# Attention with top-32 masking and two expert layers: three weight loads moved in SP's queue, and the first tiles' bound array made by ScalarE and TensorE

## The chip, the core and the metric

One core of a Trainium2 chip runs the whole program; the metric is the device time of one execution in microseconds (us). The engines are PE (TensorE, matrix products; PEld is its weight load), DVE (VectorE), ACT (ScalarE), POOL (GpSimd) and SP (SyncE, which here only issues DMAs). Each engine runs its own instructions in order, and they wait for each other by semaphores.

## The reference

Batch 4, 8 heads, 576 tokens, head size 64. Each query keeps its 32 highest scores; then a dense two-layer block, then a layer of eight experts of which each token takes one.

```python
scores = scale * np.matmul(q, k.transpose(0, 1, 3, 2))
kth = np.partition(scores, -top_k, axis=-1)[..., -top_k:-top_k + 1]
attn = softmax(np.where(scores >= kth, scores, -1e9))   # top_k = 32
x = (attn @ v) as 2304 tokens x 512
h = x @ w_in;  x = (h * np.clip(h + 3, 0, 6) / 6) @ w_out     # 512 -> 2048 -> 512
e = argmax(x @ w_gate);  out = gate * (np.maximum(x @ w1[e], 0) @ w2[e])
```

The dense block's weights come as 64-bit floats, and the kernel makes 32-bit ones of them itself.

## The kernel before, in words

The program has three stages that overlap. The **attention** runs over 144 tiles of 128 queries by 576 keys. The **dense block** runs over 144 groups (9 blocks of 256 tokens by 16 slices of the hidden layer), about one group for each tile as soon as a block of tokens is there; the rest of the groups follows the last tile. Then come the **experts**.

One attention tile t goes through these steps. `qk` (line 630) makes the scores in `sps` on PE; `sevac` copies them to `sbuf` on ACT (line 300, a helper's line), of which there are five. `top_a` takes on DVE the eight best of each eighth (line 660, tile `cd`) and from those the 24 best in three rounds (lines 666 and 671, tiles `m` and `cw`). `top_c` makes a bound `u` just under the 24th best (ACT, line 684). Then the scores above `u` are taken out and the best eight of what is left are found: `z8` (line 731, DVE). From tile 20 on (`ZPE = 20`) DVE takes them out in SBUF (`top_z`, line 696). For the first 20 tiles, when PE and the PSUM space `yps2` of the dense block are free, PE does it: `z_pe` lets POOL write an array `zw` (line 703) that holds -2^100 where the score is above `u` and 0 elsewhere, and `qk(t, zw)` makes the scores a second time in `yps2`, with the array added by a product with an identity, `identb`. That is this text's "second score product".

`act_sign` (line 721, ACT) counts for every tile how many scores lie above `u`: it writes sign(u - s) into `jk` and sums it into `sg`. `mask` compares `sg` with a table (line 735) to see which of the eight is the 32nd best, and zeroes the weights below it (line 739). Then follow the transposes (`ptps`, line 755), the product with the values (line 789) and the evacuation (lines 802 to 839).

Beside this run **32 conversions** of weight pieces, `conv64`: SP loads a 512 KB piece into `raw` (three buffers, line 316), ACT squares it and takes a sign in `sq` (lines 328 and 333), DVE builds the 32-bit words in `cvs` by three instructions (lines 329, 336 and 339), and POOL splits them (lines 298 and 347). About one conversion goes with each tile. The first three loads carry a tiny POOL copy from the scores of tile 0 (line 315), which keeps them from starting before those are there.

The order on each engine is made by the Tile scheduler from priorities: `pr(name)` sets `tc.cur_priority` to the place in the loop plus a number from the table `PRIO`, and the lowest goes first among what is ready in its plan. So a changed dependency moves rows on every engine.

Of the kernel before, what the change touches and what calls it, by code (L numbers as in the profile page):

```python
# [13 lines left out]
F32 = mybir.dt.float32  # L14
F32R = mybir.dt.float32r
BF16 = mybir.dt.bfloat16
# [41 lines left out]
def attention_two_moe_kernel(  # L58
# [95 lines left out]
    def pr(name, least=0):  # L154
        tc.cur_priority = max(least, pr0[0] + PRIO[name])
# [72 lines left out]
    def body(cs, exact, ends=None):  # L228
# [79 lines left out]

        def conv64(src, a_, nm, parts):
            n_ = DM // a_  # L310
            pr("load", pbase + 8 * len(wload))
            raw = m1p.tile([P, a_, n_, 2], U32, tag="ysb", bufs=NRAW, name=f"raw{nm}")
            if nm in ("i0", "o0", "i1"):

                G.tensor_copy(raw.rearrange("p a n t -> p (a n t)").bitcast(F32)[:, 0:1], ts[0]["s"][:, 0:1])
            SP.dma_start(raw.rearrange("p a n t -> p a (n t)"), src)
            yield
            lo, hi = raw[:, :, :, 0], raw[:, :, :, 1]
            wf = m1p.tile([P, DM], F32, tag="cvs", bufs=3, name=f"cv{nm}").rearrange("p (a n) -> p a n", a=a_)
            wb = wf.bitcast(U32)  # L320
            hf = hi.bitcast(F32)
            sq = ap1.tile([P, S], F32 if exact else BF16, tag="z" if exact else "jk", bufs=2 if exact else 1,
                          name=f"sq{nm}")[:, 0:DM].rearrange("p (a n) -> p a n", a=a_)
            pr("conv")
            if CSQ:
                G.tensor_tensor(sq, hf, hf, op=ALU.mult)
            else:
                A.activation(sq, hf, AF.Square)
            V.tensor_scalar(wb, hi, 3, 0x3FFFFFFF, op0=ALU.logical_shift_left, op1=ALU.bitwise_and)
            if not exact:  # L330
                i = wcnt[0]
                wcnt[0] += 1
                A.activation(sq, sq, AF.Sign, bias=cs["ntiny"], scale=1.0, accum_out=csum[:, i:i + 1])
            yield
            pr("conv")
            V.scalar_tensor_tensor(wb, hi, 0xC0000000, wb, op0=ALU.bitwise_and, op1=ALU.bitwise_or)
            yield
            pr("conv")
            V.scalar_tensor_tensor(wb, lo, 29, wb, op0=ALU.logical_shift_right, op1=ALU.bitwise_or)
            if exact:  # L340
                G.tensor_scalar(sq, sq, TINY2, None, op0=ALU.is_ge)
                G.tensor_tensor(wf, sq, wf, op=ALU.mult)
            yield
            pr("conv")
            h, l, done = parts()
            copy(CH, h, wf)
            G.tensor_tensor(l, wf, r_(h), op=ALU.subtract)
            done()
# [34 lines left out]
        def conv_upto(i):  # L383
            while cdone[0] <= i:
                run(conv_next())
# [1 line left out]

        identb = []
        if not exact:
            identb.append(ap1.tile([P, P], BF16, name="identb"))  # L390
            G.tensor_copy(identb[0], ident)
        NPB, NSB, VB = 3, 3 + LA, 2


# [210 lines left out]
        def qk(t, zw=None):  # L605
            pr("qk" if zw is None else "zpe")
            n, o = tiles[t]
            b, p = visits[n][:2]
            st = qx[n]
            kt = kx[b, p]  # L610
            for half in range(2):
                dst = (sps if zw is None else yps2)[:, half, 0:HS]
                if o == "T":

                    fw = visits[n][3] // P * P
                    mm = []
                    for i in st:
                        mm.append((dst, i[:, 0, fw:fw + P], kt[0][:, half * HS:(half + 1) * HS]))
                        a_, b_ = half * HS, min((half + 1) * HS, N4)
                        mm.append((dst[:, 0:b_ - a_], i[:, 1, fw:fw + P], kt[1][:, TAIL + a_:TAIL + b_]))  # L620
                        if half:
                            mm.append((dst[:, b_ - a_:HS], i[:, 1, fw:fw + P], kt[1][:, 0:TAIL]))
                else:
                    h, j = o
                    js = slice(j * P, (j + 1) * P)
                    mm = [(dst, i[:, h, js], kt[h][:, half * HS:(half + 1) * HS]) for i in st]
                if zw is not None:
                    mm.insert(0, (dst, identb[0], zw[:, half * HS:(half + 1) * HS]))
                for i, (d_, a_, b_) in enumerate(mm):
                    PE.matmul(d_, a_, b_, start=(i == 0), stop=(i == len(mm) - 1))  # L630

# [66 lines left out]
        def z_pe(t):  # L698
            if exact or not 0 <= t < ZPE:
                return  # L700
            pr("zw")
            zw = ap1.tile([P, S], F32, tag="z", bufs=2, name=f"z{t}").bitcast(BF16)[:, 0:S]
            G.tensor_scalar(zw, ts[t]["s"][:, 0:S], ts[t]["u"], -HUGE, op0=ALU.is_gt, op1=ALU.mult)
            qk(t, zw)

        def act_exp(t):
            pr("exp")
# [6 lines left out]
        def act_sign(t):  # L714
            if exact:
                return
            pr("sign")
            d = ts[t]
            jk = ap1.tile([P, S], BF16, tag="jk", bufs=1, name=f"jk{t}")
            d["sg"] = ap1.tile([P, 1], F32, tag="sg", bufs=3, name=f"sg{t}")  # L720
            A.activation(jk, d["s"][:, 0:S], AF.Sign, bias=ts[t]["u"], scale=-1.0, accum_out=d["sg"])  # L721

        def mask(t):
            if not 0 <= t < T:
                return
            d = ts[t]
            if not exact:
                pr("max8")
                z8 = ap1.tile([P, 8], F32, tag="z8", bufs=3, name=f"z8_{t}")
                j8 = ap1.tile([P, 8, 2], F32, tag="j8", bufs=1, name=f"j8_{t}")  # L730
                V.max(z8, d["z"])  # L731
                A.activation(zall[:, t:t + 1], z8[:, 1:2], AF.Sign, bias=ts[t]["u"], scale=-1.0)
                yield
                pr("match")
                V.scalar_tensor_tensor(j8, psum_isum, d["sg"], z8.unsqueeze(2).to_broadcast([P, 8, 2]), op0=ALU.is_equal, op1=ALU.mult,  # L735
                                       accum_out=tall[:, t:t + 1])
                yield
            pr("mask")
            V.scalar_tensor_tensor(d["p"], d["s"], tall[:, t:t + 1], d["p"], op0=ALU.is_ge, op1=ALU.mult)  # L739
            if tiles[t][1] == "T":  # L740

                lo, hi = d["pb"][:, N4:S], d["pb"][:, S:SW]
                copy(True, hi[TAIL:P], lo[TAIL:P])
                G.memset(lo[TAIL:P], 0.0)
                G.memset(hi[0:TAIL], 0.0)
            yield
# [355 lines left out]
        for t in range(T + 7):  # L1102
# [17 lines left out]
                pv(t - 5)  # L1120
            if t + LA < T:
                sevac(t + LA)
            if 0 <= t - 5 < T:
                xevac(t - 5)
            xg = None
# [334 lines left out]
```

## Time and profile before

| | before |
|---|---|
| median of 3 runs | 1199.83 us (1197.64 to 1202.85) |
| the profiled execution's own time | 1204.39 us |
| its span | 1202.5 us |
| busy share PE / DVE / ACT / POOL | 93% / 78% / 67% / 38% |
| POOL's array pass of the first 20 tiles | 48.6 us of POOL's busy time |
| last mask of the attention starts at | 863.3 us |

The profile's first part gives each engine's busy time. The windows view cuts the span into stretches with their own busy times and TensorE clock (granted share: 1.00 is 2.4 GHz, and values between 0.5 and 1 are stretches that mix the levels of 1.2 and 2.4 GHz). The timeline lists instructions by time, with the idle time of the engine before each in brackets and what ended it.

### The profile page before, as it was taken

The page shows a single profiled execution, that of the slowest core. Times are in us where ns is not written, and L with a number is a line of the kernel's source. Part 1 is how long each engine was busy: PE and PEld are TensorE (multiplying, and loading weights), DVE is VectorE, ACT ScalarE, POOL GpSimd, SP SyncE. Part 2 cuts the span into 40 slices and gives each one's busy share as a digit, 9 for nine tenths or more (in the row PEclk, how much of TensorE's full clock was granted, in tenths as well). Part 3 has the DMA queues.
Part 4 walks back from the last instruction along what each step waited for, and adds up shares of the span by engine and source line. Part 5 has one row for each costly group of instructions (what it writes and reads, how often), then busy time and mean ns, then how long its engine had stood idle before and what let it go on. Part 6 is the DMA issues. An engine that isn't in the chain of part 4 may idle for free.

```text
span 1202.5 us, 24061 instructions
## 1 busy us (share of the span) xinstructions
PE 1118.5 (93%) x7414; PEld 1003.8 (83%) x7414; DVE 940.9 (78%) x3853; ACT 807.6 (67%) x2082; POOL 458.5 (38%) x668
## 2 busy tenths in 40 slices
PE   5677688999999999999999999999999899999995
PEld 4566577778999989999988899999888799888885
DVE  5989989999999999998999899999641554545540
ACT  4777877778878788778778788777541353444441
POOL 5877646644332354433342432322344311222110
PEclk9668879999999999999999999999999899999998
DMA  3654456564553555754444554543486555455530
GB/s 76 189 179 142 143 171 221 162 174 125 157 134 113 151 134 142 177 135 135 118 122 126 133 147 125 152 133 110 127 271 163 176 187 179 161 176 185 160 121 31
DMA packets 184123, 179.24 MB, mean 149 GB/s; under 512 B 123629, under 2 KB 148509, under 8 KB 183984
## 3 DMA queue, kind: packets, MB, share of 16 engines
q1 hardware_dynamic: 178960, 167.24, 48.3%
q0 software_dynamic: 3872, 10.08, 2.6%
q8 instruction: 61, 1.00, 0.4%
q14 instruction: 78, 0.64, 0.2%
q10 hardware_dynamic: 1152, 0.28, 0.1%
HBM read 159.53 MB, written 18.61 MB: 148 GB/s over the span
## 4 chain that ended last, share of the span: by engine, by line
PE 71%; DVE 16%; issue 5%; ACT 4%; POOL 2%; DMA 2%; SPq 0%; POOLq 0%; ACTq 0%; DVEq 0%
PE l1ps L863 15%; PE yps L894 13%; PE ptps L789 9%; PE lp L1263 8%; PE ops L1286 8%; PE sps L630 6%; PE ptps L755 4%; DVE cd L660 2%; DVE pbuf L739 2%; DVE z L696 2%; DVE z L731 1%; PE ptps L935 1%; DVE m L666 1%; DVE cw L671 1%; PE misc L474 1%
## 5 line engine op out<-in xcount | busy, mean ns | idle before, releaser
L894 PE MATMUL yps<-wo,gh 128*128 128x512 f32 x544 | 206.7, 418 | 0.1
L298 POOL TENSOR_SCALAR gh<-gf 128x256 fp32r<-128x256 f32 x144 | 72.7, 505 | 345.2 <-PE yps L894 196.0
L660 DVE MAX8 cd<-sbuf 128x8 f32<-128x72 f32 x1152 | 187.9, 218 | 3.4 <-ACT sbuf L300 3.2
L863 PE MATMUL l1ps<-xh,wih 128*128 128x256 f32 x576 | 167.6, 291 | 4.7 <-DVE gf L875 3.1
L863 PE MATMUL l1ps<-xh,wil 128*128 128x256 f32 x576 | 164.0, 285 | 0.0
L863 PE MATMUL l1ps<-xl,wih 128*128 128x256 f32 x576 | 163.9, 285 | 0.0
L789 PE MATMUL ptps<-vn,pt 128*128 128x65 f32 (+1 forms) x1152 | 145.8, 281 | 0.0
L789 PEld LDWEIGHTS ptps<-vn,pt 128*128 128x128 f32 x1152 | 143.0, 201 | 0.0
L739 DVE SCALAR_TENSOR_TENSOR pbuf<-sbuf,tall,pbuf 128x576 f32<-128x576 f32 x144 | 136.8, 950 | 0.1
L883 POOL TENSOR_TENSOR gl<-gf,gh 128x256 fp32r<-128x256 f32 x144 | 125.5, 871 | 11.4
L863 PEld LDWEIGHTS l1ps<-xh,wih 128*128 128x128 f32 x576 | 110.4, 192 | 14.9 <-DVE gf L875 7.6
L1036 DVE TENSOR_TENSOR wl<-raw,wh 128x1024 fp32r<-128x1024 f32 x64 | 78.6, 1236 | 53.7 <-ACT wh L1035 51.6
L721 ACT ACTIVATE jk<-sbuf,uall 128x576 bf16<-128x576 f32 x144 | 111.6, 775 | 4.2 <-DVE j L735 0.9
L863 PEld LDWEIGHTS l1ps<-xl,wih 128*128 128x128 f32 x576 | 110.6, 192 | 4.2
L712 ACT ACTIVATE pbuf<-sbuf,nb 128x576 f32<-128x576 f32 x144 | 111.2, 775 | 4.1 <-PE ptps L757 0.9
L894 PEld LDWEIGHTS yps<-wo,gh 128*128 128x128 f32 x544 | 101.2, 190 | 14.8 <-POOL qh L486 0.3
L300 ACT ACTIVATE sbuf<-sps 128x576 f32<-128x576 f32 x144 | 92.9, 645 | 30.4 <-PE sps L630 16.5
L869 ACT ACTIVATE gf<-l1ps,three 128x256 f32<-128x256 f32 x144 | 67.9, 471 | 66.9 <-PE l1ps L863 55.7
L755 PE MATMUL ptps<-ident,pbuf 128*128 128x128 f32 x576 | 93.9, 286 | 19.7 <-DVE j L735 12.6
L894 PE MATMUL yps<-wo,gl 128*128 128x512 f32 x272 | 110.4, 406 | 0.6 <-POOL gl L883 0.6
L863 PEld LDWEIGHTS l1ps<-xh,wil 128*128 128x128 f32 x576 | 110.6, 192 | 0.1
L630 PE MATMUL sps<-kx,qh 128*128 128x288 f32 (+2 forms) x336 | 96.8, 319 | 14.3 <-ACT sbuf L300 10.5
(259 smaller groups left out, 2974.7 us busy)
## 6 DMA issues: line engine op xcount, KB each, us to landing
wo<-wod SPq DMA_DIRECT2D x144, 512.0 KB, 3.8
raw<-in_moe_w_dram SPq DMA_DIRECT2D x64, 512.0 KB, 4.3
vn<-in_v_dram SPq DMA_DIRECT2D x96, 128.0 KB, 2.7
rawi<-in_moe_w_in_dram SPq DMA_DIRECT2D x16, 512.0 KB, 4.0
rawo<-in_moe_w_out_dram SPq DMA_DIRECT2D x16, 512.0 KB, 4.6
wod<-wc SPq DMA_DIRECT2D x16, 512.0 KB, 5.6
qn<-in_q_dram SPq DMA_DIRECT2D x126, 64.0 KB, 2.5
yd<-y SPq DMA_DIRECT2D x18, 258.0 KB, 5.1
```

The lines of the kernel that those rows point to most:

```text
L630: PE.matmul(d_, a_, b_, start=(i == 0), stop=(i == len(mm) - 1))
L660: V.max(cd[:, c, :], s[:, c * CK:(c + 1) * CK])
L712: A.activation(d["p"], d["s"], AF.Exp, bias=d["nb"], scale=SCALE)
L721: A.activation(jk, d["s"][:, 0:S], AF.Sign, bias=ts[t]["u"], scale=-1.0, accum_out=d["sg"])
L739: V.scalar_tensor_tensor(d["p"], d["s"], tall[:, t:t + 1], d["p"], op0=ALU.is_ge, op1=ALU.mult)
L755: PE.transpose(ptps[:, c * P:(c + 1) * P], pb[:, c0 + c * P:c0 + (c + 1) * P], ident)
L789: PE.matmul(d_, a_, b_, start=(i == 0), stop=(i == len(mm) - 1))
L863: PE.matmul(dst, a[:, c, fs], b_[:, c, :], start=(n == 0), stop=(n == 3 * NCC - 1))
L883: G.tensor_tensor(gl, gf, r_(gh), op=ALU.subtract)
L894: PE.matmul(acc(bk, tt), a[:, tsl], b_, start=(f == 0 and m == 0), stop=(f == NF1 - 1 and m == 2))
L1263: PE.matmul(lp, a[:, c, fs], b_[:, c, 0:w], start=(n == 0), stop=(n == 3 * NCC - 1))
L1286: PE.matmul(ops_[j][0:n], a, b_[:, ns], start=(f == 0 and i == 0), stop=(f == NF2 - 1 and i == len(ms) - 1))
```

## The change

Five edits. (1) Pieces `i0`, `o0` and `i1` are loaded at a priority ahead of everything else in the load class, and their conversions are called in the first round of the loop, at the priority `match`. A tiny POOL copy from the scores of tile 2 now holds their `cvs` and `sq` buffers until that tile is there. (2) `sq` lies in the two buffers tagged `z` and no longer in the one buffer of `jk`. (3) For tiles 0 to 19, POOL's array pass is gone. PE reads `jk` in its place: -2^99 times a field of ones (`below`) plus 2^99 times sign(u - s) gives 0 for a score under the bound and -2^100 for one above it. There are now four products for each half of the second score product, where there were three. (4) The sign pass of those tiles takes the priority `zw`. (5) The comparison with the table uses one column in place of two for those tiles.

```diff
         def conv64(src, a_, nm, parts):
             n_ = DM // a_
-            pr("load", pbase + 8 * len(wload))
+            early = nm in ("i0", "o0", "i1")
+            pr("load", 0 if early else pbase + 8 * len(wload))
+            if early:
+                tc.cur_priority -= 100
             raw = m1p.tile([P, a_, n_, 2], U32, tag="ysb", bufs=NRAW, name=f"raw{nm}")
-            if nm in ("i0", "o0", "i1"):
-
+            if early:
                 G.tensor_copy(raw.rearrange("p a n t -> p (a n t)").bitcast(F32)[:, 0:1], ts[0]["s"][:, 0:1])
...
-            sq = ap1.tile([P, S], F32 if exact else BF16, tag="z" if exact else "jk", bufs=2 if exact else 1,
-                          name=f"sq{nm}")[:, 0:DM].rearrange("p (a n) -> p a n", a=a_)
-            pr("conv")
+            sq = ap1.tile([P, S], F32, tag="z", bufs=2, name=f"sq{nm}")
+            sq = (sq if exact else sq.bitcast(BF16))[:, 0:DM].rearrange("p (a n) -> p a n", a=a_)
+            ck = "match" if early else "conv"
+            if early:
+                pr("load")
+                for x in (wf, sq):
+                    G.tensor_copy(x.rearrange("p a n -> p (a n)")[:, 0:1], ts[2]["s"][:, 0:1])
+            pr(ck)
...
-            identb.append(ap1.tile([P, P], BF16, name="identb"))
-            G.tensor_copy(identb[0], ident)
+            for i, a_ in enumerate((HUGE / 2, -HUGE / 2)):
+                identb.append(ap1.tile([P, P], BF16, name=f"identb{i}"))
+                G.tensor_scalar(identb[i], ident, a_, 0.0, op0=ALU.mult, op1=ALU.add)
+            below = ap1.tile([P, HS], BF16, name="below")
+            G.memset(below, 1.0)
...
-                    mm.insert(0, (dst, identb[0], zw[:, half * HS:(half + 1) * HS]))
+                    mm[0:0] = [(dst, identb[1], below), (dst, identb[0], zw[:, half * HS:(half + 1) * HS])]
...
-            pr("zw")
-            zw = ap1.tile([P, S], F32, tag="z", bufs=2, name=f"z{t}").bitcast(BF16)[:, 0:S]
-            G.tensor_scalar(zw, ts[t]["s"][:, 0:S], ts[t]["u"], -HUGE, op0=ALU.is_gt, op1=ALU.mult)
-            qk(t, zw)
+            qk(t, ts[t]["jk"])
...
-            pr("sign")
+            pr("sign" if t >= ZPE else "zw")
...
+                w_ = 1 if t < ZPE else 2
...
+            if t == 0:
+                conv_upto(1)
```

**Where rows move on DVE, start of the program.** Before, between the rounds of tile 1 (`m_1`, `cw_319`) and the first `z8` (`z_0`), only the eighths of tile 2 (`cd_395`) stood:

```order
L666 MAX m_1_317<-cw_319 128x8
L660 MAX cd_395<-sbuf_158 128x8
L671 MATCH_REPLACE cw_319<-m_1_317,cw_319 128x64
L660 MAX cd_395<-sbuf_158 128x8
L666 MAX m_1_317<-cw_319 128x8
L660 MAX cd_395<-sbuf_158 128x8 x6
L731 MAX z_0_406<-yps 128x8
```

Now the conversions of three pieces (`cvi_269`, `cvi_361`, `cvo_282`) stand there; these are the first rows of it, and the last:

```order
L676 MAX m_1_349<-cw_351 128x8
L336 TENSOR_SCALAR cvi_269<-rawi_236 128x512
L681 MATCH_REPLACE cw_351<-m_1_349,cw_351 128x64
L343 SCALAR_TENSOR_TENSOR cvi_269<-rawi_236,cvi_269 128x512
L676 MAX m_1_349<-cw_351 128x8
L346 SCALAR_TENSOR_TENSOR cvi_269<-rawi_236,cvi_269 128x512
L336 TENSOR_SCALAR cvi_361<-rawi_242 128x512
...
L346 SCALAR_TENSOR_TENSOR cvo_282<-rawo_239,cvo_282 128x512
L670 MAX cd_429<-sbuf_162 128x8 x4
L738 MAX z_0_440<-yps 128x8
```

So nine DVE instructions moved ahead of the first `z8`.

**Where rows move on SP's queue.** Before, the last load of the second pair's queries (`qn_222`) stood right behind that pair's keys (`kd_1`), then seven loads of values, the third pair's keys and queries, and only then the first two weight pieces:

```order
L515 DMA kd_1_208<-in_k_dram 128x4x64 x2
L528 DMA qn_222<-in_q_dram 128x2x64
L549 DMA vn_161<-in_v_dram 128x4x64
...
L515 DMA kd_2_293<-in_k_dram 128x4x64 x2
L516 DMA ke_2_294<-in_k_dram 64x64 x2
L528 DMA qn_370<-in_q_dram 128x2x64 x4
L550 DMA vp_164<-in_v_dram 64x64
L316 DMA rawi_232<-in_moe_w_in_dram 128x4x256
L316 DMA rawo_235<-in_moe_w_out_dram 128x1024
```

Now three pieces stand behind `kd_1`, and the last load of the second pair's queries (`qn_226`) stands behind the third pair's keys (`kd_2`, `ke_2`):

```order
L525 DMA kd_1_212<-in_k_dram 128x4x64 x2
L318 DMA rawi_236<-in_moe_w_in_dram 128x4x256
L318 DMA rawi_242<-in_moe_w_in_dram 128x4x256
L318 DMA rawo_239<-in_moe_w_out_dram 128x1024
L559 DMA vn_165<-in_v_dram 128x4x64
L525 DMA kd_2_325<-in_k_dram 128x4x64 x2
L526 DMA ke_2_326<-in_k_dram 64x64 x2
L538 DMA qn_226<-in_q_dram 128x2x64
```

The weight pieces moved ahead by two pairs' loads, and one load of queries moved back behind four loads of keys.

## Rows read from the trace of the kernel before

**Rows 1.** Windows view; columns: stretch, length, busy PE, PEld, DVE, ACT, POOL, clock, DMA.

```profile
15.00:33.00 18.00, 14.10 (x58) 11.08 (x59) 12.94 (x74) 11.24 (x29) 12.77 (x13) 0.91 0.46 120
33.00:60.00 27.00, 15.48 (x76) 13.26 (x75) 27.00 (x71) 21.09 (x53) 23.80 (x22) 0.69 0.64 175
60.00:150.00 90.00, 65.21 (x376) 56.06 (x376) 83.38 (x346) 72.86 (x192) 63.44 (x46) 0.78 0.52 155
300.00:860.00 560.00, 553.72 (x4068) 510.77 (x4068) 521.37 (x2442) 444.32 (x1246) 192.15 (x319) 1.00 0.51 136
```

**Rows 2.** Timeline of DVE, 18 to 36 us: start, duration, instruction, idle before.

```profile
18.28 0.21 DVE L666 MAX8 m<-cw 128x8 f32<-128x64 f32 x1
...
22.22 0.77 DVE L731 MAX8 z<-yps 128x8 f32<-128x576 f32 x1 [2.93 <-PE yps L630]
...
28.64 0.77 DVE L731 MAX8 z<-yps 128x8 f32<-128x576 f32 x1 [0.94 <-PE yps L630]
...
32.58 0.24 DVE L660 MAX8 cd<-sbuf 128x8 f32<-128x72 f32 x1 [0.66 <-ACT sbuf L300]
...
33.45 0.89 DVE L329 TENSOR_SCALAR cvi<-rawi 128x512 uint32<-128x512 uint32 x1
...
34.40 0.67 DVE L336 SCALAR_TENSOR_TENSOR cvi<-rawi,cvi 128x512 uint32<-128x512 uint32 x1
...
35.17 0.71 DVE L339 SCALAR_TENSOR_TENSOR cvi<-rawi,cvi 128x512 uint32<-128x512 uint32 x1
```

**Rows 3.** DMA issues: size of one, median us from issue to landing.

```profile
rawi<-in_moe_w_in_dram SPq DMA_DIRECT2D x16, 512.0 KB, 4.0
...
qn<-in_q_dram SPq DMA_DIRECT2D x126, 64.0 KB, 2.5
```

**Rows 4.** Timeline of SP's queue, 13 to 26 us.

```profile
13.14 0.62 SPq L528 DMA_DIRECT2D qn<-in_q_dram  x1
...
23.11 1.22 SPq L515 DMA_DIRECT2D kd<-in_k_dram  x2
```

**Rows 5.** Groups of instructions, 0 to 150 us, shapes apart: busy us, mean ns | idle before.

```profile
L703 POOL TENSOR_SCALAR z<-sbuf,uall 128x576 bf16<-128x576 f32 x20 | 48.6, 2429 | 10.6 <-ACT uall L684 9.3
...
L329 DVE TENSOR_SCALAR cvi<-rawi 128x512 uint32<-128x512 uint32 x10 | 7.6, 758 | 0.0
```

**Rows 6.** Timeline of POOL and then DVE, 97 to 106 us.

```profile
97.44 2.21 POOL L703 TENSOR_SCALAR z<-sbuf,uall 128x576 bf16<-128x576 f32 x1
...
102.16 1.28 POOL L347 TENSOR_TENSOR wil<-cvi,wih 128x512 fp32r<-128x512 f32 x1
103.54 2.77 POOL L703 TENSOR_SCALAR z<-sbuf,uall 128x576 bf16<-128x576 f32 x1
...
97.58 0.87 DVE L329 TENSOR_SCALAR cvi<-rawi 128x512 uint32<-128x512 uint32 x1
...
99.05 0.80 DVE L739 SCALAR_TENSOR_TENSOR pbuf<-sbuf,tall,pbuf 128x576 f32<-128x576 f32 x1
...
102.59 1.47 DVE L739 SCALAR_TENSOR_TENSOR pbuf<-sbuf,tall,pbuf 128x576 f32<-128x576 f32 x1
...
105.39 0.40 DVE L329 TENSOR_SCALAR cvo<-rawo 128x512 uint32<-128x512 uint32 x1
```

**Rows 7.** DVE's groups with idle time before them, 15 to 150 us.

```profile
L839 DVE TENSOR_TENSOR xl<-misc,xh 128x128 fp32r<-128x128 f32 x8 | 2.3, 284 | 4.1 <-ACT xh L835 4.1
...
L802 DVE TENSOR_SCALAR rs<-ptps 128x2 f32<-128x2 f32 x8 | 1.2, 151 | 2.5 <-PE ptps L789 2.5
```

**Rows 8.** Timeline of ACT and then PE, 114 to 117 us.

```profile
114.25 0.78 ACT L721 ACTIVATE jk<-sbuf,uall 128x576 bf16<-128x576 f32 x1
...
114.72 0.46 PE L630 MATMUL yps<-z,identb 128*128 128x288 bf16 x1
...
115.47 0.46 PE L630 MATMUL yps<-z,identb 128*128 128x288 bf16 x1
...
116.21 1.06 PE L755 MATMUL ptps<-ident,pbuf 128*128 128x128 f32 x4
```

More of the change, by code (lines that the diff above doesn't have):

```diff
@@ L334, in conv64 @@
             yield
-            pr("conv")
+            pr(ck)
             V.scalar_tensor_tensor(wb, hi, 0xC0000000, wb, op0=ALU.bitwise_and, op1=ALU.bitwise_or)
             yield
-            pr("conv")
+            pr(ck)
             V.scalar_tensor_tensor(wb, lo, 29, wb, op0=ALU.logical_shift_right, op1=ALU.bitwise_or)
@@ L716, in act_sign @@
                 return
-            pr("sign")
+            pr("sign" if t >= ZPE else "zw")
             d = ts[t]
-            jk = ap1.tile([P, S], BF16, tag="jk", bufs=1, name=f"jk{t}")
+            d["jk"] = jk = ap1.tile([P, S], BF16, tag="jk", bufs=1, name=f"jk{t}")
             d["sg"] = ap1.tile([P, 1], F32, tag="sg", bufs=3, name=f"sg{t}")
@@ L734, in mask @@
                 pr("match")
-                V.scalar_tensor_tensor(j8, psum_isum, d["sg"], z8.unsqueeze(2).to_broadcast([P, 8, 2]), op0=ALU.is_equal, op1=ALU.mult,
-                                       accum_out=tall[:, t:t + 1])
+                w_ = 1 if t < ZPE else 2
+                V.scalar_tensor_tensor(j8[:, :, 0:w_], psum_isum[:, :, 0:w_], d["sg"], z8.unsqueeze(2).to_broadcast([P, 8, w_]),
+                                       op0=ALU.is_equal, op1=ALU.mult, accum_out=tall[:, t:t + 1])
                 yield
```

## The prediction

> **What bounds the kernel now.** I read the windows view first, because the share of the whole span says little about a kernel of three stages [rows 1]. From 300 to 860 us PE is busy 553.7 of 560 us at the full clock and DVE 521.4. From 33 to 60 us DVE is busy 27.0 of 27 us, while PE has 15.5. From 60 to 150 us it is DVE 83.4 and PE 65.2 of 90. So the first 150 us, where the change lies, are DVE's, and PE waits there. The order of the tiles is fixed and each tile brings one group of the dense block with it, so what DVE loses or gains before 150 us shifts everything after it. I count the change in DVE's busy and idle time, and nothing that it does to POOL alone.
>
> Second, the timeline of DVE at the start [rows 2]. DVE is through with tile 1's rounds at about 18.5 us and then waits: 2.93 us for the first `z8` at 22.22, 0.94 us for another at 28.64, and 0.66 us for scores at 32.58. That is 4.5 us. The first conversion comes only at 33.45, and from there on DVE has no hole for 27 us. The wait at 22.22 ends with PE's second score product, which waited for POOL's array pass.
>
> **Three conversions into the holes.** One conversion takes DVE 0.89 + 0.67 + 0.71 = 2.27 us [rows 2], three take 6.8 us. The order of the changed kernel puts them between tile 1's rounds and the first `z8`. Are the pieces there? A 512 KB load lands a median 4.0 us after its issue [rows 3]. SP comes to the first of them where it issued the last queries before, at 13.14 us; each issue holds the queue for 0.62 us [rows 4]. POOL's small copy must come first and needs tile 0's scores, which were there at about 13.5. So the first lands at about 13.8 + 4.0 = 17.8 us, and the others by 20. DVE gets to them at 18.5, 20.8 and 23, so it should wait for none. It then has work from 18.5 to at least 26.5 (6.8 us plus the eighths of tile 2, some 1.2 us), while the first `z8` is ready at about 22: the hole of 2.93 us is gone.
>
> What is late next is the moved load of queries. It now stands behind the third pair's keys, which SP issued at 23.11, when PE had read the keys before them [rows 4]; four key loads take 2.4 us, the query load 0.6, and it lands 2.5 us later [rows 3], at about 28.7. PE transposes it then, ACT and DVE split it at about 30. DVE has `z8`, masks and eighths of tiles 2 and 3 to fill the time up to there, about 3.4 us from 26.5 on, so I leave a hole of 0.5 us. The term is 4.5 - 0.5 = **-4.0 us**. Its ends are 0 (every hole returns elsewhere) and -4.5. If a piece lands late, each us of it is lost one for one, because the rounds of tile 1 and the first mask stand behind it on DVE.
>
> **POOL's array pass goes.** It is 48.6 us of POOL's time [rows 5], and POOL is not the bound, so the question is what it does to DVE. The rows answer it by pairs [rows 6]. While the pass ran from 97.44 to 99.65, DVE's first conversion instruction, begun right after the pass, took 0.87 us; the same one at 105.39, 1.85 us into the next pass, took 0.40. But the mask at 99.05, inside the same pass, took 0.80 us, as little as any. The mask at 102.59 took 1.47 us, under POOL's two-input subtraction (102.16 to 103.44), which stays. So the pass costs DVE 0.47 us where the first conversion instruction runs into it. I find five such meetings (at 33.45, 35.81, 97.58, 109.62 and 132.8) and a weaker one of 0.15: **-2.5 us**. Its ends: 0, and -3.6 for each of the two kinds of piece were all of the surplus over 0.40 due to it (7.6 less 10 of 0.40 [rows 5], the other kind having less), so -4.7 in all.
>
> The Trainium skill, in "SBUF — State Buffer", section "Who interferes with whom", says that a DVE instruction with two SBUF inputs contends with a GpSimd instruction that reads SBUF, and that the loser blocks fully. By that, the mask at 99.05 should have stood until 99.65, and taking away 20 passes would give back some 0.6 us at each of about 24 such meetings, 14 us in all. The trace disagrees for this pass, with 0.80 us, and agrees for the two-input subtraction, with 1.47; the measurement decides, and nothing is added for it.
>
> **PE's two added products.** One product of 288 columns takes 0.25 us from start to start at the low clock: 114.72 to 115.47 for three [rows 8]. Forty of them are 10 us at most, and PE has 25 us idle between 60 and 150 us [rows 1]; the field of ones does not wait for the sign. They cost only where DVE waits for PE. From 15 to 150 us DVE waited 4.1 us before line 839 and 2.5 us before line 802 [rows 7], both at the end of a chain through PE, in four larger holes. Two products in each hole are 0.5 us, so +2.0 at most and 0 at least. I take one hole in four, **+0.5 us**, because most of PE's wait is for the previous `z8` and the ones could start with it. The holes themselves, 6.6 us, I leave as they are. Neither their chain nor its order on PE is undone by the change; that all of them go is the other end, -6.6.
>
> **Edits at nothing.** The sign pass was done before too and takes 0.78 us [rows 8]; that it comes earlier costs nothing as long as ACT, busy 72.9 of 90 us, has room. That it must now wait until PE has read the one `jk` buffer is priced under the rivals. `sq` in two buffers: before tile 20 nothing else uses them, after that DVE's own array takes one in turn, which ACT and DVE leave in order. POOL's new copies, some ten small ones, lie where POOL lost 48.6 us. The table comparison at half its width: below 0.1 us each, under the noise.
>
> **Sum.** -4.0 - 2.5 + 0.5 = -6.0 us. The profiled execution took 1204.4 us, 4.6 above the median of the three runs; less 6.0 it is 1198.4, and on the scale of the median **1193.8, say 1194 us**. This is almost at 0.5% (6.0 us), which is about what a measurement of this kernel can tell from no change.
>
> **The rivals.**
> - *More goes than I count.* With the array earlier and POOL out of the chain, the holes before lines 839 and 802 close too: -6.0 - 6.6, about 1187 us. For it: the second score product stands ahead of the transposes and value products on PE, so all of that chain starts sooner. The Trainium skill ("TensorE: Matmul & The Clock Gate", "What's actually happening") says that activity releases TensorE's clock; the rows show 0.69 and 0.78 in the DVE-bound stretches, so added products could also lift it, which no run here shows yet. Against it: those holes are behind ACT and DVE waits as well.
> - *The fill is given back.* The conversions are done sooner, but DVE then stands for a later thing, the fourth weight piece behind the query loads, or the queries themselves: about 1199 us, no change. That the three loads do not land in time, so that the change does not do what it says, ends here too.
> - *Slower: the single `jk` buffer.* ACT may write tile t+1's sign only after PE has read tile t's. In the rows ACT wrote a sign at 114.25, while PE read the array of an earlier tile from 114.72 to 116.21 [rows 8]. Bound that way, ACT would stand 2.0 us, and behind the sign stand score copies and exponentials that DVE needs. ACT has 17.1 us idle in the 90 [rows 1], about 1.1 us for each of some 15 tiles, so 0.9 us would be uncovered: 13 us over those tiles, less the gain of 6.0, about 1207 us. It decides where the wait is over about 1.1 us a tile. Against it: PE waits for the `z8` before, so it usually reads soon after the sign.
>
> **How the numbers follow.** Forecast 0.52, from -3 to -9 us, half of it beyond 0.5%; more goes 0.20, all faster; given back 0.15, all the same; slower 0.13. So faster 0.26 + 0.20 = 0.46, the same 0.26 + 0.15 = 0.41, slower 0.13. The range: down to all lower ends, -4.5 - 4.7 - 6.6 = -15.8, which is 1184, with 1 us for the orders that the scheduler makes anew further on: 1183. Up to +2.0 for the products with no gain, 1202, and 1 us more: 1203. Of the forecast's own case it is 1190 to 1197.
>
> **What would show it.** Right: no hole of DVE over 1 us between 18 and 36 us, the first conversion at about 18.5 us, the first `z8` at about 27; the first conversion instruction at 0.40 us in nearly all places; masks under the subtraction still at about 1.5 us; the last mask some 6 us before 863. Wrong: DVE waiting for a `raw` landing or for `ql`; idle time on ACT before the sign pass (line 728 now) that ends with PE; the stretch from 300 to 860 us longer by several us, since the scheduler moved rows there as well.

## The result, and the profile after

| | before | changed |
|---|---|---|
| median of 8 runs each | 1199.14 us (1197.64 to 1203.63) | 1210.21 us (1205.58 to 1215.12) |
| ratio, 95% interval | | 1.0085 (1.0063 to 1.0107) |
| the profiled execution's own time, its span | 1204.39 us, 1202.5 us | 1215.12 us, 1213.2 us |
| last mask of the attention starts at | 863.28 us | 873.14 us |

The changed kernel is slower, where the forecast was 6 us faster, and the time is outside the range (1183 to 1203). A second measurement on another occasion gave 1.0057 (1.0038 to 1.0076), so the loss is 7 to 10 us. Both profiled executions are slow ones of their kernel (5 us above the median of the eight runs each), so distances between the two traces hold to a few us only, and the steps from tile to tile say more than their level.

The windows view of the changed kernel, with the columns of [rows 1] and one stretch more:

```profile
15.00:33.00 18.00, 11.79 (x44) 9.01 (x45) 15.77 (x63) 13.13 (x34) 13.26 (x21) 0.81 0.54 152
33.00:60.00 27.00, 18.52 (x95) 15.99 (x94) 24.99 (x80) 21.15 (x53) 14.05 (x17) 0.63 0.63 180
60.00:150.00 90.00, 66.09 (x413) 56.29 (x413) 84.11 (x358) 73.58 (x197) 31.04 (x33) 0.86 0.54 166
150.00:240.00 90.00, 78.09 (x460) 70.32 (x459) 81.13 (x306) 62.88 (x165) 42.48 (x60) 0.83 0.51 169
300.00:860.00 560.00, 552.50 (x4030) 509.26 (x4029) 519.52 (x2418) 441.83 (x1240) 183.62 (x315) 0.99 0.49 134
```

Against [rows 1], POOL has lost 32.4 us between 60 and 150 us, as its pass is gone. DVE has 2.8 us more work done between 15 and 33 us. These are the things that the change set out to do. What was not foreseen stands in the two lower lines: DVE has 8.9 us without work from 150 to 240 us, and TensorE's clock, 1.00 in [rows 1] from 300 to 860 us, is 0.99 there and 0.83 from 150 to 240. In the kernel before, DVE has 3.6 us without work there, and the clock is 0.91:

```profile
150.00:240.00 90.00, 80.23 (x504) 69.46 (x504) 86.42 (x329) 68.52 (x184) 50.47 (x66) 0.91 0.58 185
```

The timeline of DVE from 17 to 37 us, and of POOL in the same stretch, to be read against [rows 2]:

```profile
18.71 0.48 DVE L336 TENSOR_SCALAR cvi<-rawi 128x512 uint32<-128x512 uint32 x1 [0.95 <-POOL cvi L330]
...
23.21 1.61 DVE L343 SCALAR_TENSOR_TENSOR cvo<-rawo,cvo 128x512 uint32<-128x512 uint32 x1
...
26.30 0.74 DVE L738 MAX8 z<-yps 128x8 f32<-128x576 f32 x1
...
30.82 0.69 DVE L502 TENSOR_TENSOR ql<-misc,qh 128x512 fp32r<-128x512 f32 x1 [1.09 <-ACT qh L492]
...
36.71 0.77 DVE L738 MAX8 z<-yps 128x8 f32<-128x576 f32 x1 [1.26 <-PE yps L640]
22.81 1.46 POOL L354 TENSOR_TENSOR wil<-cvi,wih 128x512 fp32r<-128x512 f32 x1
```

The first conversion begins at 18.71 us, the first `z8` at 26.30, and the hole of 2.93 us is gone. But conversions that follow each other closely meet POOL's subtraction of the piece before: the instruction at 23.21 stood 1.61 us instead of 0.67, under POOL's row at 22.81. And DVE waits 1.09 us at 30.82 for the queries that were loaded later, where the prediction left a hole of 0.5.

**Where the time went.** I took the start of DVE's mask of every tile from both traces and subtracted. By these two traces the changed kernel is 2.0 us *ahead* at tile 24, and 9.9 us behind at the last tile. Nearly all of that comes in four steps: +8.5 us from tile 24 to 30 (of which 5.2 are back at tile 32), +2.4 from tile 32 to 46, +2.2 from tile 64 to 70, +5.8 from tile 100 to 110. No row of the change is there. The first step, in the timelines of DVE, POOL and PE:

```profile
222.65 1.84 DVE L706 SCALAR_TENSOR_TENSOR z<-sbuf,uall 128x576 f32<-128x576 f32 x1
224.41 0.41 DVE L502 TENSOR_TENSOR ql<-misc,qh 128x256 fp32r<-128x256 f32 x1
222.61 1.26 POOL L354 TENSOR_TENSOR wc<-cvo,wc 128x512 fp32r<-128x512 f32 x1
224.87 0.61 PE L640 MATMUL sps<-kx,ql 128*128 128x288 f32 x1 [2.90 <-DVE ql L502]
...
227.90 3.52 PE L797 MATMUL ptps<-vn,pt 128*128 128x65 f32 x16
```

PE stands 2.90 us for the low parts `ql` of the queries. On DVE these stand behind the last piece's conversion and an array `z` that took 1.84 us under POOL's subtraction. Behind the hole TensorE's granted clock is half (224.3 to 234.5 us in the records), and 16 value products take 3.52 us.

### The profile page after: what moved, and what is told of

Read it like the earlier page. It is cut to its first block, busy times and chain, and to the rows that moved or that the text cites. A ratio compares the mean times of both kernels' runs of the same rounds, so it can differ in the third digit from the quotient of the medians.

```text
span 1213.2 us, 24083 instructions
## 1 busy us (share of the span) xinstructions
PE 1127.8 (93%) x7454; PEld 1014.6 (84%) x7454; DVE 943.5 (78%) x3853; ACT 808.3 (67%) x2082; POOL 403.1 (33%) x656
## 4 chain that ended last, share of the span: by engine, by line
PE 69%; DVE 16%; ACT 5%; issue 5%; DMA 3%; POOL 1%; SPq 0%; POOLq 0%; DVEq 0%; ACTq 0%
PE l1ps L871 14%; PE yps L902 12%; PE ptps L797 10%; PE lp L1273 8%; PE ops L1296 8%; PE sps L640 5%; PE ptps L763 4%; DVE cd L670 3%; DVE pbuf L747 2%; DVE z L706 2%; DVE z L738 2%; DVE m L676 1%; PE yps L640 1%; DVE cw L681 1%; DMA kd<-in_k_dram 1%
## 5 line engine op out<-in xcount | busy, mean ns | idle before, releaser
L797 PE MATMUL ptps<-vn,pt 128*128 128x65 f32 (+1 forms) x1152 | 148.5, 284 | 0.0
L797 PEld LDWEIGHTS ptps<-vn,pt 128*128 128x128 f32 x1152 | 145.5, 204 | 0.0
L747 DVE SCALAR_TENSOR_TENSOR pbuf<-sbuf,tall,pbuf 128x576 f32<-128x576 f32 x144 | 139.6, 970 | 0.1
L891 POOL TENSOR_TENSOR gl<-gf,gh 128x256 fp32r<-128x256 f32 x144 | 119.8, 832 | 11.4
L763 PE MATMUL ptps<-ident,pbuf 128*128 128x128 f32 x576 | 92.9, 285 | 16.2 <-DVE j L743 11.1
L300 ACT ACTIVATE sbuf<-sps 128x576 f32<-128x576 f32 x144 | 93.3, 648 | 20.3 <-PE sps L640 15.1
```

The source lines that it names most:

```text
L763: PE.transpose(ptps[:, c * P:(c + 1) * P], pb[:, c0 + c * P:c0 + (c + 1) * P], ident)
L891: G.tensor_tensor(gl, gf, r_(gh), op=ALU.subtract)
```

## The experiments

Theory 1: the two conversions that come early move every later piece by two places; the scheduler orders the rows behind tile 24 anew, and this order costs about 10 us. Theory 2: `sq` in the `z` buffers holds DVE up after tile 20. Theory 3: PE's two added products and the single `jk` buffer. Each kernel below was timed in five rounds beside the kernel before, which had a median of 1201.46 us in the first four runs, 1203.13 in the next four and 1202.54 in the last four.

**1. The early loads and conversions alone** (POOL's pass, `sq` in `jk` and the old products stay):

```diff
+            early = nm in ("i0", "o0", "i1")
+            pr("load", 0 if early else pbase + 8 * len(wload))
...
+            if t == 0:
+                conv_upto(1)
```

> The kernel before with the first part of the change alone: three raw pieces loaded behind the second pair's keys, and two whole conversions ahead of tile 0's eighths; POOL's array pass, the one jk buffer for sq and the old products stay. Its order of rows differs from the kernel before all the way to the last tiles. Theory 1 (the two conversions that come early move every later piece by two places, the scheduler then orders the rows after tile 24 anew, and that order costs about 10 us): slower than before by 6 to 12 us, about 1207, and the loss comes after the mask of tile 24. Theory 2 (sq in DVE's z buffers holds up DVE after tile 20) and theory 3 (PE's two added products and the one jk buffer): both are absent here, so 1193 to 1200.

Measured 1208.52 us, ratio 1.0060 (1.0042 to 1.0079). As theory 1 has it, and without anything of theories 2 and 3. The place of the loss is as expected too, by its trace: the masks stand 0.2 us behind those of before at tiles 19 to 28, 3.3 ahead at tile 32, 3.5 behind at the end.

**2. The other parts alone** (array from the sign pass, scaled diagonal, `sq` in `z`; loads and conversions as before):

```diff
-            zw = ap1.tile([P, S], F32, tag="z", bufs=2, name=f"z{t}").bitcast(BF16)[:, 0:S]
-            G.tensor_scalar(zw, ts[t]["s"][:, 0:S], ts[t]["u"], -HUGE, op0=ALU.is_gt, op1=ALU.mult)
-            qk(t, zw)
+            qk(t, ts[t]["jk"])
```

> The kernel before with the other parts alone: the array of the first 20 tiles from ACT's sign and the scaled diagonal, and sq in the z buffers; loads and conversions where they were before. From about tile 24 on its rows stand as in the kernel before. Theory 1: faster than before by 0 to 4 us, about 1197 (my 2.5 us for POOL's pass less 0.5 for the products), and the masks of tiles 24 to 143 keep one distance from those of before. Theory 2: slower by 3 to 6 us, lost between tiles 20 and 34. Theory 3: slower by over 5 us, lost in the first 20 tiles, with ACT idle before the sign until PE is through.

Measured 1200.83 us, ratio 0.9997 (0.9983 to 1.0011): no loss, so theories 2 and 3 fall, and no gain either, where I had -2.0. (Its profiled execution took 1197.84 us, 3.0 less than its median; that of before took some 3 more than its own. Distances between these two traces say 6 us too much, so I go by the medians.)

**3. The changed kernel, rejoined.** A count (`cacc`, 15 more per tile, a piece at every 16) gives out the conversions. It starts two pieces lower, so the two early ones are made up for at once:

```diff
-        cacc = 0
+        cacc = -32
```

> The changed kernel whole, but the count that gives out later conversions starts two pieces lower, so that after the two early ones the next come where they came before. All parts of the change stay (early loads, two early conversions, sign array, sq in z). From about tile 24 on the rows stand as in the kernel before but for a few. Theory 1: the 10 us that the changed kernel lost after tile 24 are not lost; what is left is the early gain, so 1193 to 1198, 1.2% faster than the changed kernel. Theories 2 and 3: all that they blame is still here, so about 1208 to 1210 as the changed kernel.

Measured 1196.44 us, ratio 0.9960 (0.9947 to 0.9973). All edits are in, and it is 5.0 us faster than before. This one number is worth 12 to 15 us to the changed kernel. That is what theory 1 says of the places of the pieces; where the loss arises, runs 9 and 10 tell. The last mask of the rejoined kernel, then that of the changed one:

```profile
854.27 0.82 DVE L747 SCALAR_TENSOR_TENSOR pbuf<-sbuf,tall,pbuf 128x576 f32<-128x576 f32 x1
```

```profile
873.14 0.82 DVE L747 SCALAR_TENSOR_TENSOR pbuf<-sbuf,tall,pbuf 128x576 f32<-128x576 f32 x1
```

**4. The changed kernel without the early conversions** (the loads stay early):

```diff
-            if t == 0:
-                conv_upto(1)
```

> The changed kernel without the call that does two conversions ahead of tile 0's eighths; the three raw pieces are still loaded early, the sign array and sq in z stay. The pieces are then given out as before, and the rows after tile 24 stand as in the kernel before but for a few. Theory 1: 1195 to 1200: no late loss, but less of the early gain, since DVE's holes before 33 us are empty again. Theories 2 and 3: about 1208 to 1210. If it is as fast as the run that keeps the two early conversions and puts later ones back, the filled holes are worth nothing.

Measured 1198.15 us, ratio 0.9975 (0.9956 to 0.9994): no late loss. The two conversions in the holes are worth 1.7 us beside run 3, less than the intervals can tell apart.

**5. The kernel before, its pieces two places ahead:**

```diff
-        cacc = 0
+        cacc = 32
```

> The kernel before, of the change nothing but that two conversions are given out at once at the start, so that every later piece comes two places earlier; its rows after the first tiles stand almost as in the changed kernel. Theory 1 (the places of the pieces and the order that follows from them): slower than before by 5 to 10 us, with the loss after tile 28, most of it between tiles 98 and 110. If instead the early loads, the sign array or sq in z are needed for the loss (theories 2 and 3): 1199 to 1202, no change.

Measured 1213.74 us, ratio 1.0092 (1.0067 to 1.0117). The size is as theory 1 has it, the place is not: without the early loads DVE waits for the pieces at the start, its mask of tile 0 is 23.9 us later than before, and of this 11 us stay to the end. From tile 28 on it loses nothing more, on balance (10.9 us behind at tile 28, 10.0 at the last tile). So this run speaks against theory 1 as it was put: behind tile 29's mask DVE's rows stand word for word as in the changed kernel, and that order alone cost nothing here. What its profile does not have is the half clock, below.

**6. The changed kernel again.**

> The changed kernel, nothing else, beside the others on one chip and with a second profile. Theory 1: 1208 to 1212, with the same holes of PE at the same tiles (2 to 3 us before tile 29's mask, 1.2 us before tile 102's) in this execution too, and TensorE at half the clock behind the one at tile 102 as in the run with the loads alone. Against it: a half clock at other tiles with the same total, since then the place would be chance and not the order.

Measured 1209.40 us, ratio 1.0057 (1.0038 to 1.0076). The holes are back at the same tiles, 2.90 us ahead of tile 29's mask and 1.24 us ahead of tile 102's, each with half the clock behind it for 6.8 us. The step from tile 64 to 70 of the first profile, with a half clock at 429 us, is only 0.7 us here, and without one.

**7. The tail as before.** The eighths of one tile are asked for later; the scheduler then goes back to the old order from tile 73 on:

```diff
+            if t == 50:
+                tc.cur_priority += 250
             for c in range(NCK):
```

> The changed kernel with one number more: the eighths of tile 50 are asked for 250 steps of priority later. Up to tile 45 every row of DVE stands as in the changed kernel, from tile 73 on as in the kernel before, so the hole of PE at tile 102 (1.23 us, TensorE at half clock for 6.8 and 10.2 us behind it) is gone and all that comes ahead of tile 45 is still there. Theory 1: 5 to 6 us faster than the changed kernel, about 1204, the masks of tiles 110 to 143 at the distance from before that tile 73 has. If the loss lies all ahead of tile 45, or in the clock by chance: 1208 to 1212 as the changed kernel.

Measured 1207.47 us, ratio 1.0044 (1.0027 to 1.0060). In the profile the hole at tile 102 is gone, and from tile 100 to 110 the kernel takes 1.8 us more than before, against 5.7 in run 6. The medians are only 1.9 us apart, less than expected. So the step at tile 102 is real in the profiles, but it is not shown that it costs as much in most executions. The record has TensorE's mean granted clock of every timed execution: run 7's profiled one has 0.966, the highest of its twelve, and their median is 0.959, no higher than run 6's 0.961.

**8. Three early conversions,** made up for:

```diff
-        cacc = 0
+        cacc = -48
...
-                conv_upto(1)
+                conv_upto(2)
```

> The run that puts the later pieces back, with three conversions forced ahead of tile 0's eighths instead of two and the later ones starting three pieces lower: from tile 31 on the rows of DVE stand as in the kernel before. Theory 1: 1193 to 1198, as good as with two or better by up to 2 us, since DVE has no conversion to do in the first tiles after that. If three conversions are too many for the holes, 1197 to 1200.

Measured 1196.72 us, ratio 0.9955 (0.9935 to 0.9974): with run 3 the fastest version, 6.4 us under before.

**9 and 10. Early and late apart.** Run 9 is the changed kernel to tile 9, and as before from tile 32's mask on; run 10 is the rejoined one to tile 9, and then as the changed one. The two edits at tile 12, of the changed and of the rejoined kernel:

```diff
             cacc += CRATE
+            if t == 12:
+                cacc -= 32
```

```diff
             cacc += CRATE
+            if t == 12:
+                cacc += 32
```

> The changed kernel up to tile 9, row by row on DVE; at tile 12 the count of conversions is set two pieces back, and from tile 31 on the rows stand as in the kernel before. By the profiles so far the changed kernel stands 13 us behind the rejoined one: some 11 of it at tile 10 (4.5 the two conversions' own work, the rest not), 2.6 given back by tile 32, 1.9 lost again from tile 32 to 44 and 4.4 from tile 100 to 110. If that holds (theory 1 in two parts): the early 6 us stay, the late ones go: 1203 to 1206 where before takes 1201 to 1203. If all the loss comes after tile 24, as I first thought: 1196 to 1198. If all of it comes early: 1208 to 1210.

> The rejoined kernel up to tile 9 (two early conversions, then none for two pieces), and at tile 12 the count is set two pieces ahead, so that from there on the rows stand as in the changed kernel. In two parts: 1201 to 1205, the late 5 to 7 us are lost, the early ones not. If all the loss comes late: 1208 to 1210. If all of it comes early: 1196 to 1198.

Measured 1200.22 us, ratio 0.9989 (0.9972 to 1.0005), and 1204.12 us, ratio 1.0016 (0.9991 to 1.0040). With runs 3 and 6 this makes a square (median less that of before, us):

| | later pieces as before | two places ahead |
|---|---|---|
| start as in the rejoined kernel | -5.0 (run 3) | +1.6 (run 10) |
| start as in the changed kernel | -2.3 (run 9) | +6.3 (run 6) |

The later places cost 6.6 and 8.6 us, the start 2.7 and 4.7. So by the medians about two thirds of the loss comes late and one third early. Each of these steps is uncertain by 3 to 4 us, by the runs' intervals, and the first measurement of the changed kernel (+11.1 in place of +6.3) would make them 13.4 and 9.5 where run 6 enters. (Run 10 does the two pieces at tile 12 and not at the start, so their own work lies in its late part: by the table below it is 5.4 us behind run 3 at tile 10, and from tile 28 to 32, where those pieces are missing, gets 0.3 back.) Run 10 is as expected. Run 9 is below what the split by profiles gave, 1203 to 1206: I had put too much on the early part.

The distances of the masks from those of before show the same in the profiles (start of the mask of a tile, less that in the trace of before, us; only the steps down a column count):

| tile | changed | run 6 | run 7 | run 3 | run 9 | run 10 |
|---|---|---|---|---|---|---|
| 10 | -0.6 | 0.8 | -1.0 | -10.1 | 0.8 | -4.7 |
| 24 | -2.0 | -3.4 | -5.3 | -13.3 | -6.6 | -8.7 |
| 28 | 0.3 | -3.6 | -5.5 | -10.9 | -6.8 | -8.8 |
| 30 | 6.5 | 1.4 | -0.6 | -10.8 | -6.7 | -3.9 |
| 32 | 1.3 | -3.8 | -5.8 | -11.1 | -7.0 | -9.1 |
| 46 | 3.7 | -1.0 | -3.1 | -10.6 | -6.6 | -6.4 |
| 100 | 4.7 | -1.1 | -3.7 | -10.2 | -3.8 | -7.3 |
| 110 | 10.5 | 4.6 | -1.9 | -9.0 | -2.7 | -1.7 |
| 143 | 9.9 | 4.0 | -1.9 | -9.0 | -2.7 | -2.4 |

Runs 3 and 9 keep their distance to within 0.7 us from tile 28 to 46, where the late order makes a peak at tile 30 and loses 2.4 to 2.8 us from tile 32 to 46.

**11 and 12. POOL's subtraction with one input,** in the changed and in the rejoined kernel:

```diff
-            G.tensor_tensor(l, wf, r_(h), op=ALU.subtract)
+            G.tensor_scalar(l, wf, 1.0, 0.0, op0=ALU.mult, op1=ALU.add)
```

> The changed kernel with POOL's subtraction of each converted piece (two inputs, 1.3 us) replaced by a single-input pass over the same piece; PE's, DVE's and ACT's rows stand word for word as in the changed kernel. The low parts of the dense block's weights are not computed. If DVE's long conversions and masks under that subtraction are a cause of the early loss: 5 to 10 us faster than the changed kernel, about 1202, the second and third conversion instructions at 0.7 us instead of up to 1.8, and the gap to the next run is under 10 us instead of 13. If they are not (the places of the pieces alone count): within 2 us of the changed kernel, 1208 to 1210.

> The rejoined kernel with the same replacement, again without the low parts of the weights; DVE's rows stand as in the rejoined kernel. Its profile has 10 us of DVE's surplus under that subtraction up to tile 32, the changed kernel's 13.4. If contention counts: 1189 to 1193, 4 to 7 us faster than the rejoined kernel. If it does not: 1195 to 1198.

Measured 1204.84 us, ratio 1.0021 (1.0001 to 1.0041), and 1196.02 us, ratio 0.9960 (0.9944 to 0.9976). The changed kernel gains about 4 us on run 6, between the two forecasts, and the rejoined one nothing. DVE's surplus (each instruction's time over the tenth percentile of its form, where that is over 0.05 us, summed from 15 to 215 us) falls from 17.9 to 8.7 us in the one and from 14.2 to 5.8 in the other; but its idle time rises from 13.7 to 18.3 and from 10.6 to 15.1. About half of what contention frees is taken by the next wait. So contention is a part of the changed kernel's loss, and the gap between the two that stays, 0.6%, is not what the second input costs. How much of the 4 us is contention itself and how much the shorter hole at tile 29 that comes with it (2.06 us, below), the runs do not tell.

The Trainium skill ("SBUF — State Buffer", "Who interferes with whom") says that a DVE instruction with two SBUF inputs contends with a GpSimd instruction that reads SBUF. For the subtraction the runs agree, and for the pass with one input too. In run 11 an array `z` begun inside that pass took 1.18 us instead of 0.80 and ended 0.61 us after it:

```profile
157.52 1.18 DVE L706 SCALAR_TENSOR_TENSOR z<-sbuf,uall 128x576 f32<-128x576 f32 x1
157.47 0.62 POOL L354 TENSOR_SCALAR wc<-cvo 128x512 fp32r<-128x512 f32 x1
```

The mask under the subtraction in [rows 6] did the same: begun at 102.59, it ended 0.62 us behind the subtraction. The pass with one input lasts half as long, 0.70 us on average against 1.41, and DVE's surplus under it fell from 14.3 to 6.2 us, in about the same measure. So runs 11 and 12 halve the contention and do not remove it. POOL's array pass of before, in which a mask took 0.80 us [rows 6], is the one that did not hold DVE's masks up.

**The clock behind a hole.** The same rows of PE at tile 102 in run 6, with the windows view behind them:

```profile
637.38 0.33 PE L763 MATMUL ptps<-ident,pbuf 128*128 128x128 f32 x1 [1.24 <-DVE j L743]
...
639.75 3.52 PE L797 MATMUL ptps<-vn,pt 128*128 128x65 f32 x16
636.00:642.00 6.00, 4.76 (x24) 4.21 (x23) 3.81 (x22) 3.45 (x14) 0.53 (x3) 0.70 0.12 38
```

in run 5:

```profile
648.01 0.33 PE L755 MATMUL ptps<-ident,pbuf 128*128 128x128 f32 x1 [1.23 <-DVE j L735]
...
649.76 1.90 PE L789 MATMUL ptps<-vn,pt 128*128 128x65 f32 x16
646.00:652.00 6.00, 4.69 (x33) 3.88 (x34) 4.76 (x29) 4.10 (x15) 0.67 (x4) 1.00 0.21 77
```

and in run 7, without the hole:

```profile
635.65 1.90 PE L799 MATMUL ptps<-vn,pt 128*128 128x65 f32 x16
630.00:636.00 6.00, 5.58 (x35) 4.20 (x35) 5.91 (x28) 5.59 (x16) 2.05 (x6) 1.00 0.28 87
636.00:642.00 6.00, 5.86 (x47) 5.48 (x47) 5.80 (x27) 4.53 (x14) 1.63 (x5) 1.00 0.33 95
```

The hole comes from PE's order. In the kernel before and in the changed one DVE takes six eighths ahead of the table comparison, which reads `ptps`, and PE's next transposes into `ptps` wait for it. Before, PE has a product more of the dense block and the transposes of `qn` to do ahead of them, and no hole:

```profile
637.18 0.89 DVE L660 MAX8 cd<-sbuf 128x8 f32<-128x72 f32 x6
638.10 0.23 DVE L735 SCALAR_TENSOR_TENSOR j<-ptps,sg,z 128x16 f32<-128x16 f32 x1
...
637.13 0.40 PE L894 MATMUL yps<-wo,gh 128*128 128x512 f32 x1
637.60 0.33 PE L474 MATMUL misc<-ident,qn 128*128 128x128 f32 x1
...
638.52 0.66 PE L755 MATMUL ptps<-ident,pbuf 128*128 128x128 f32 x4
```

In the changed kernel the first transposes into `ptps` stand ahead of those of `qn`, and PE waits with nothing else to do:

```profile
641.95 0.89 DVE L670 MAX8 cd<-sbuf 128x8 f32<-128x72 f32 x6
642.88 0.23 DVE L743 SCALAR_TENSOR_TENSOR j<-ptps,sg,z 128x16 f32<-128x16 f32 x1
...
641.55 0.40 PE L902 MATMUL yps<-wo,gl 128*128 128x512 f32 x1
643.17 0.33 PE L763 MATMUL ptps<-ident,pbuf 128*128 128x128 f32 x1 [1.23 <-DVE j L743]
643.34 0.27 PE L484 MATMUL misc<-ident,qn 128*128 128x128 f32 x1
```

Run 5 has the same hole and the same rows as run 6, and the full clock: 16 products take 1.90 us and not 3.52. From tile 100 to 110 it takes 1.1 us more than before, run 6 5.7, the changed kernel's first profile 5.8. Runs 2, 3, 4, 8 and 9, which have before's order there and no such hole, take 1.1 to 1.5 us more as well. So the hole by itself cost nothing that shows, and the half clock behind it some 4.6 us.

The same at the other hole. In run 1 it is shorter, and the clock stays full:

```profile
224.74 0.40 PE L637 MATMUL sps<-kx,ql 128*128 128x288 f32 x1 [1.83 <-DVE ql L499]
...
226.34 1.90 PE L796 MATMUL ptps<-vn,pt 128*128 128x65 f32 x16
```

Runs 1 and 5 (1.83 us both) get 3.5 and 3.4 us back from tile 28 to 32, where the two pieces done early are missing; with the half clock, runs 6, 7 and 10 get back 0.2 to 0.3, and the changed kernel's first profile loses 1.0. Run 11 lies between: a hole of 2.06 us, the half clock for 3.4, and 2.1 us back.

All the profiles together, from the mask of tile 28 to that of tile 143:

| profiles | half clock in between, us | time in between, less that of before, us |
|---|---|---|
| runs 3, 4 and 8 (before's order) | none | 1.6 to 1.9 |
| runs 2, 9 and 12 (before's order) | 3.4 | 4.0 to 4.1 |
| run 5 (late order) | none | -0.9 |
| run 7 (late order up to tile 73) | 6.8 | 3.6 |
| run 1 (late order) | 10.2 | 3.3 |
| runs 10 and 6 (late order) | 13.7 | 6.5 and 7.5 |
| run 11, changed (late order) | 17.1, 20.5 | 8.1, 9.6 |

The time goes with the half clock, 0.4 to 0.7 us for each us of it against the profiles of the same order without it. The late order without it (run 5) is not slower than before, if the 3.4 us are counted that the two pieces done early give back. So in the profiles the late loss is the clock's, and the order's part in it is that it makes the holes. Each line is one to three executions, and no run changed the clock and left the order as it was.

## Why the prediction was wrong

**The bound** was read rightly for the first 150 us. What failed is the sentence drawn from it, that what DVE gains before 150 us shifts everything after it. That holds only if the rows behind stay as they are. They do in runs 2, 3, 4, 8 and 9, where DVE's order is that of before from tile 32's mask on, and PE's from tile 34's on. In the changed kernel both differ to the last tiles.

**Three conversions into the holes, -4.0.** The holes did close: DVE waited 4.9 us between 18 and 36 us before, 2.0 in the first profile after and 1.4 in the second. The load order worked; at 18.71 DVE waited 0.95 us for POOL's small copy, not for a landing. But I did not ask where the conversions that were pulled ahead would be missing. The count goes on giving out a piece at nearly every tile, so tiles 1 to 28 had as much conversion to do as before, and the gain could come only where the pieces run out, at tiles 28 to 32. There PE's hole and the half clock took it. With the pieces put back, the term is about -1.7 us for two conversions (run 3 against run 4) and -3.1 for three, which it was priced for (run 8 against run 4, each less its own before); neither is clear of the intervals.

**POOL's pass, -2.5, and the products, +0.5.** Together the array part gave -0.4 us (run 2; the interval reaches from -2.0 to +1.3), so -2.0 is at its edge. The first conversion instruction became shorter, 0.62 us on average before and 0.47 in the first profile after (0.55 in the second) from 17 to 100 us, without the part that runs beside the next instruction. But the second and third became longer or stayed, 0.72 before, 0.78 and 0.72 after; at 23.21 one is seen to meet the subtraction of the piece before.

**The early loads** without the conversions, which I had not priced apart, are worth some 2.7 us by the medians (run 4 against run 2, with intervals that overlap).

**The sum** of these parts was nearly right: -6.0 predicted, -5.0 in run 3 and -6.4 in run 8. That is partly luck, since some 2.7 us of it come from the early loads, which had no price, and the array part gave next to nothing. The term that was mis-sized, and the step that failed, is "1 us for the orders that the scheduler makes anew further on". It is 7 to 9 us by the square, and in the profiles it is the half clock behind PE's new holes. The 3 to 5 us of the start, where the conversions crowd the first tiles, had no term at all. I had named the later orders among the signs of a wrong prediction ("the stretch from 300 to 860 us longer by several us"), and had seen rows move up to the last tiles, but gave it no case and no chance of its own.

**The rivals.** *More goes*: the holes before lines 839 and 802 did shrink, but a new one before the queries' low parts takes their place:

```profile
L502 DVE TENSOR_TENSOR ql<-misc,qh 128x512 fp32r<-128x512 f32 x6 | 4.1, 684 | 3.5 <-ACT qh L492 3.5
...
L847 DVE TENSOR_TENSOR xl<-misc,xh 128x128 fp32r<-128x128 f32 x8 | 2.3, 289 | 1.8 <-ACT xh L843 1.7
...
L810 DVE TENSOR_SCALAR rs<-ptps 128x2 f32<-128x2 f32 x8 | 1.2, 152 | 1.7 <-PE ptps L797 1.7
```

against 4.1 and 2.5 us in [rows 7]. *The fill is given back* describes the first 28 tiles well, but stops there. *Slower by the single `jk` buffer* named nearly the right time (1207 us) for a wrong reason, by luck. The wait is there, as the group of the sign pass from 15 to 150 us shows:

```profile
L728 ACT ACTIVATE jk<-sbuf,uall 128x576 bf16<-128x576 f32 x22 | 16.9, 770 | 5.2 <-PE yps L640 5.0
```

Run 2 has 4.8 us of it from 60 to 150 us and is no slower than before, so ACT's slack covered it, as the forecast assumed.

## What to carry to other kernels

Where work is pulled ahead, ask at which place it will be missing, and whether the engine that gains there is still the bound; a count or a rate that goes on as before gives the gain back until the work runs out. Where a scheduler makes the order anew, put the moved rows' places back (here one number, -32), so that the order behind is the known one, and compare the orders of all engines: the hole at tile 102 is in PE's rows, not in DVE's; a change of rows in the tail deserves its own term, of several us here, until a profile has shown otherwise. In a stretch that TensorE bounds, look for its holes of a microsecond and more together with the clock behind them.

## What was not expected of the hardware

A hole of PE in the bound stretch can cost several times its length, when TensorE goes to 1.2 GHz behind it. The hole of 2.9 us at tile 29 was followed by the half clock in all four profiles in which it had that length (changed, runs 6, 7 and 10; 6.8 to 10.2 us of it), that of 2.06 us in run 11 by 3.4 us of it, and that of 1.83 us in neither of two (runs 1 and 5). The hole of 1.2 to 1.4 us at tile 102 was followed by it in five of six (changed, runs 1, 6, 10 and 11; not run 5). At tile 65, where nearly every version has a hole, one of 1.85 to 2.38 us was followed by 3.4 us of it in four profiles (changed, runs 2, 9 and 11), and one of 1.49 to 2.06 us was not in eight (before, runs 1, 3, 5, 6, 8, 10 and 12). So the length does not decide alone, and before's order is not free of it. The Trainium skill ("TensorE: Matmul & The Clock Gate", "What's actually happening") says that the clock follows how busy the engine has been lately, which fits. That filling the hole with other products would hold the clock was not tried. Where in the timed executions the half clock lay, their times and mean clocks do not tell.
